# The first load in two halves: x tile 0 from two queues, and the loads behind it moved on ScalarE's queue

## The chip, the cores and the metric

The kernel runs on one core of one Trainium2 chip, in one launch. The metric is the device time in microseconds. The trace comes from one profiled execution; times without a profile come from repeated runs. The engines are TensorE (PE; its weight loads are shown as PEld), VectorE (DVE), ScalarE (ACT), GpSimd (POOL) and SyncE (SP). SyncE, ScalarE and GpSimd also issue DMAs; in the packet lists SyncE's queue is q1 and ScalarE's is q10.

## The reference

```python
def _A_ref(x, wqkv, w_phi, wo):              # S=2048 tokens, D=448, 16 heads of 28
    q, k, v = split_heads(x @ wqkv)
    pq, pk = q @ w_phi, k @ w_phi            # per head
    phi_q = concat(softmax(pq), softmax(-pq))
    phi_k = concat(softmax(pk), softmax(-pk))
    kv  = einsum("bhsf,bhsd->bhfd", phi_k, v)
    z   = einsum("bhsf->bhf", phi_k)
    num = einsum("bhqf,bhfd->bhqd", phi_q, kv)
    den = einsum("bhqf,bhf->bhq", phi_q, z) + 1e-6
    return merge_heads(num / den) @ wo

def _B_ref(x, w1, w2):                       # w1 448x1792, w2 1792x448
    return silu(x @ w1) @ w2

xn = layernorm(x)                            # over D, eps 1e-5
return x + _A_ref(xn, ...) + _B_ref(xn, ...)
```

Everything is bf16; the input x is (1, 2048, 448).

## The kernel before

The 2048 tokens are 16 tiles of 128 rows (x tile t, 112 KB each). Tiles 0 to 3 are loaded one by one, the rest in blocks of four. Each tile is normalised on VectorE (`ln_tile`, L717): statistics (`bnst`, L720), mean and variance (`bnag`, L721), the reciprocal of the root (`rstd`, L726; the root itself, `ve`, L724, runs on ScalarE for tiles 0 to 3), and the normalised tile (`xn`, L735). Tiles 0 to 3 are then transposed on TensorE (`tr`, L539) into PSUM and copied out to `xnT` by ScalarE (`ev`, L545), tile 3 by VectorE; later tiles are transposed by DMA. On `xnT` the first feed-forward product starts at once, for tokens 0 to 511, in pieces per tile (L522): `00a` is block 0 on tile 0, first two steps.

The program is written as a list of operations with the ranges they read and write. A planner (`schedule`, L228) books each on its engine with a duration from small formulas and a landing time for loads, and so fixes each engine's order; semaphore waits follow from the ranges. `chain` (L1036) adds order edges by name, within one engine. The order of TensorE is wholly written out: the word list at L1062 for the head, a plan string (L361) for the rest. For VectorE's head it is L1047, for ScalarE's L1048.

Before any data arrive, 36 matmuls on a constant run on TensorE (L588, traced as L589), and an `act` on `ones_bf` (L568, named `warm_act`) brings ScalarE's square-root table in; the planner books it with n = 2050, where `d_act(n)` (L509) is n/1.2 + 60 ns. `ones_bf` is set by a GpSimd memset named `ones`.

The first loads (L605 to L608): x tile 0 from SyncE, then tiles 1, 2 and 3 from ScalarE. Behind tile 0 SyncE issues the blocks of `w1` (traced as `phT`, in whose space they lie), then the other weights and x blocks, which wait for nothing. On ScalarE the order is x1, x2, the table warm-up, x3; and x1 waits for `ones` (L1050):

```python
chain("bnst0 bnag0 bnst1 rstd0 bnag1 xn0 rstd1 xn1 bnst2 bnag2 bnst3 bnag3 rstd2 xn2 ...".split())
chain("x1 x2 warm_act x3 ve0 ve1 ev0a ev0 ev1a ev1 ve2 ve3 ev2a ev2 silu_table".split())
byname["x1"].deps.add(byname["ones"].id)
for name, lat in (("x1", 2000.0), ("x2", 2800.0), ("x3", 2200.0)):
    byname[name].xfer, byname[name].lat = 0.0, lat
```

So tile 1's statistics stand ahead of xn0 on VectorE, and tile 2's behind xn1. The last two of these lines are the planner's landing times for x1, x2 and x3.

Of the kernel before, what the change touches and what calls it, by code (L numbers as in the profile page):

```python
# [370 lines left out]
def bass_parallel_sum__linear_kernel_hedgehog__dense_activation_silu__prompt_kernel(  # L371
# [29 lines left out]
    def rows_of(a, t0, t1):  # L401
        for u0, u1 in TILES:
            if u0 <= t0 < u1:
                v = a[0][128 * u0:128 * u1, :].rearrange("(p t) d -> p t d", p=128)
                return v[:, t0 - u0:t1 - u0, :]
# [3 lines left out]
    with es:  # L409
        def sb(name, shape, dt):  # L410
            return es.enter_context(nc.sbuf_tensor(name, shape, dt))

        x_sb = sb("x_sb", [128, NT, D], BF16)
# [64 lines left out]
        warm_act = sb("warm_act", [128, 4], F32)  # L478
# [76 lines left out]
        def load(dst, src, name, eng="sp", lat=1700.0):  # L555
            n = 2
            for _, cnt in list(dst.ap):
                n *= cnt
            P.dma(lambda e: e.dma_start(out=dst, in_=src), n / 280.0, writes=[dst], name=name, eng=eng, lat=lat)
# [35 lines left out]
        def load_x(t0, t1, eng="sp"):  # L595
            load(x_sb[:, t0:t1, :], rows_of(A_x, t0, t1), f"x{t0}", eng, lat=1400.0)
# [5 lines left out]
        def load_w1(c0, c1, eng="sp"):  # L602
            load_rows4(w1_sb[:, :, c0:c1], B_w1, c0, c1, f"w1_{c0}", eng)

        load_x(0, 1)  # L605
        load_x(1, 2, "act")
        load_x(2, 3, "act")
        load_x(3, 4, "act")  # L608
# [427 lines left out]
        def chain(names):  # L1036
            byname = {o.name: o for o in P.ops}
            for a, b in zip(names, names[1:]):
                byname[b].odeps.add(byname[a].id)
                byname[b].odeps -= byname[b].deps  # L1040
# [4 lines left out]
        fold()  # L1045
        act(warm_act[:], ones_bf[:, 0:4], ACTF.Silu, 4, "silu_table", table="silu", okeys_w=["sq"])
        chain("bnst0 bnag0 bnst1 rstd0 bnag1 xn0 rstd1 xn1 bnst2 bnag2 bnst3 bnag3 rstd2 xn2 rstd3 xn3 ev3".split())  # L1047
        chain("x1 x2 warm_act x3 ve0 ve1 ev0a ev0 ev1a ev1 ve2 ve3 ev2a ev2 silu_table".split())  # L1048
        byname = {o.name: o for o in P.ops}
        byname["x1"].deps.add(byname["ones"].id)  # L1050
        for name, lat in (("x1", 2000.0), ("x2", 2800.0), ("x3", 2200.0)):
            byname[name].xfer, byname[name].lat = 0.0, lat
        fold_loads()
# [239 lines left out]
```

## Time and profile before

| | us |
|---|---|
| median of 3 runs | 144.71 (144.23, 144.71, 145.35) |
| the profiled execution | 144.79, of which the span is 143.5 |
| TensorE busy | 140.7 (98% of the span) |
| VectorE, ScalarE, GpSimd busy | 90.3, 79.6, 78.8 |
| x tile 0: issued, landing after | 0.80, 2.1 |
| x tile 1: issued, landing after | 1.04, 2.1 |
| first w1 block (256 KB): issued, landing after | 1.27, 3.9 |
| x tile 2 and x tile 3: landing after | 3.7 and 3.7 |

Times of instructions count from the span's start. A timeline row gives the start, the length from first to last of a merged group, engine, line, operation, output and inputs, the number of instructions, and in brackets the idle time ahead of it and what ended it. A merged row of two loads covers both. A matmul's row ends when its result is out; matmuls overlap, so their number in a stretch tells more than the busy share.

### The profile page before, as it was taken

Reading aid. Unit: us, or ns where it says so; the run is one execution under the profiler, and the core shown is the slowest. Engines: PE = TensorE matmul, PEld = TensorE weight load, DVE = VectorE, ACT = ScalarE, POOL = GpSimd, SP = SyncE. Lnnn points to the kernel's source line nnn. Section 1 sums busy time; section 2 is a strip of 40 time slices with the busy share of each in tenths; the row PEclk is TensorE's granted clock in tenths of the full one; section 3 lists DMA queues with packets and bytes.
Section 4 is the critical chain, followed back from the end, with each engine's and each line's share of the span. In section 5 each row is a group of like instructions: output and inputs, shape, how many; then the busy total and the mean of one; then the engine's idle time right before and its main releaser. Section 6 shows DMA issues by size and latency. Waiting matters only on the chain.

```text
span 143.5 us, 4565 instructions
## 1 busy us (share of the span) xinstructions
PE 140.7 (98%) x1966; PEld 82.8 (58%) x1966; DVE 90.3 (63%) x194; ACT 79.6 (55%) x98; POOL 78.8 (55%) x98
## 2 busy tenths in 40 slices
PE   7999999999999999999999999999999999999994
PEld 7894444445444544476687655555555555555673
DVE  1978998700860069939049998957977564265533
ACT  4668776479996999889888948237440000000000
POOL 8948667570296009799935999991595700000000
DMA  4999998675990000000000058959589999824922
GB/s 126 328 308 262 275 165 116 117 100 95 350 286 5 0 2 5 0 0 5 0 5 5 5 106 163 138 109 159 106 164 144 215 214 162 144 49 97 181 83 64
DMA packets 45252, 17.43 MB, mean 121 GB/s; under 512 B 37024, under 2 KB 44848, under 8 KB 45232
## 3 DMA queue, kind: packets, MB, share of 16 engines
q1 hardware_dynamic: 42160, 14.35, 53.9%
q10 hardware_dynamic: 2736, 2.14, 5.8%
q0 software_dynamic: 336, 0.65, 1.3%
q8 instruction: 15, 0.25, 0.7%
q14 instruction: 5, 0.04, 0.1%
HBM read 6.40 MB, written 1.84 MB: 57 GB/s over the span
## 4 chain that ended last, share of the span: by engine, by line
PE 98%; DVE 0%; issue 0%
PE psum L522 94%; PE psum L589 3%; PE psum L539 1%; DVE x_sb L1023 0%
## 5 line engine op out<-in xcount | busy, mean ns | idle before, releaser
L522 PE MATMUL psum<-xnT,phT 64*128 64x512 bf16 (+1 forms) x428 | 47.0, 351 | 0.0
L522 PE MATMUL psum<-w_sb,hT 64*128 64x448 bf16 (+4 forms) x455 | 46.0, 340 | 0.0
L856 DVE TENSOR_REDUCE Rec<-Ek_sb 128x32 f32<-128x896 bf16 (+1 forms) x20 | 24.6, 1258 | 18.6 <-ACT Ek_sb L545 18.6
L522 PEld LDWEIGHTS psum<-w_sb,hT 64*128 64x128 bf16 (+1 forms) x455 | 23.6, 94 | 17.5 <-ACT Ek_sb L545 0.2
L545 ACT ACTIVATE hT<-psum 128x1024 bf16<-128x1024 f32 x28 | 27.6, 1024 | 10.6 <-PE psum L522 10.5
L522 PEld LDWEIGHTS psum<-xnT,phT 64*128 64x128 bf16 (+1 forms) x428 | 22.8, 95 | 17.6 <-ACT vaug L545 0.7
L893 POOL TENSOR_TENSOR RA<-Ek_sb,Rec 128x896 bf16<-128x896 bf16 x16 | 26.6, 1698 | 6.3 <-DVE Rec L857 4.7
L522 PE MATMUL psum<-Wqk,xnT 64*128 64x432 bf16 x224 | 24.6, 343 | 0.0
L545 ACT ACTIVATE Ek_sb<-psum 128x864 bf16<-128x864 f32 x24 | 20.4, 913 | 6.3 <-PE psum L522 5.4
L866 POOL TENSOR_TENSOR Ek_sb<-Ek_sb,Rec 128x896 bf16<-128x896 bf16 x8 | 13.4, 1698 | 15.9 <-DVE Rec L857 8.8
L545 ACT ACT_TABLE_LOAD x11 | 14.1, 1283 | 2.8 <-POOL Wp L552 1.9
L522 PEld LDWEIGHTS psum<-Wqk,xnT 64*128 64x128 bf16 x224 | 10.9, 94 | 8.1 <-ACT hT L545 0.4
L866 POOL TENSOR_TENSOR phT<-phT,Rec 128x896 bf16<-128x896 bf16 x8 | 13.4, 1698 | 1.2 <-issue 0.9
L522 PE MATMUL psum<-wv,xnT 64*128 64x448 bf16 x112 | 12.4, 349 | 0.0
L720 DVE BATCH_NORM_STATS2 st<-x_sb 128x6 f32<-128x448 bf16 x16 | 9.6, 602 | 2.9 <-DMA x_sb<-in_A_x_dram 2.9
L522 PE MATMUL psum<-wo_sb,vaug 64*128 64x448 bf16 (+2 forms) x102 | 11.3, 339 | 0.0
L1023 DVE TENSOR_TENSOR x_sb<-psum,x_sb 128x448 bf16<-128x448 f32 (+2 forms) x13 | 7.2, 584 | 5.6 <-PE psum L522 5.5
L735 DVE TENSOR_SCALAR RA<-x_sb,mv,rstd 128x384 bf16<-128x384 bf16 (+2 forms) x28 | 9.5, 376 | 0.7 <-POOL rstd L731 0.5
L1002 DVE TENSOR_TENSOR vaug<-psum,rden 128x448 bf16<-128x448 f32 x16 | 9.3, 620 | 0.0
L856 DVE TENSOR_REDUCE Rec<-phT 128x64 f32<-128x1792 bf16 x4 | 8.0, 1991 | 1.9 <-ACT phT L545 1.8
L857 DVE RECIPROCAL Rec<-Rec 128x32 f32<-128x32 f32 (+1 forms) x24 | 8.9, 397 | 0.2
L545 ACT ACTIVATE vaug<-psum 128x896 bf16<-128x896 f32 x8 | 7.5, 949 | 2.4 <-PE psum L522 2.4
(61 smaller groups left out, 109.3 us busy)
## 6 DMA issues: line engine op xcount, KB each, us to landing
out_dram<-x_sb ACTq DMA_DIRECT2D x15, 112.0 KB, 2.6
w_sb<-in_B_w_dram SPq DMA_DIRECT2D x1, 1568.0 KB, 7.4
x_sb<-in_A_x_dram SPq DMA_DIRECT2D x2, 448.0 KB, 6.7
wo_sb<-in_A_wo_dram SPq DMA_DIRECT2D x2, 336.0 KB, 7.2
phT<-in_B_w_dram SPq DMA_DIRECT2D x3, 192.0 KB, 5.4
x_sb<-in_A_x_dram POOLq DMA_DIRECT2D x1, 448.0 KB, 4.6
phT<-in_B_w_dram SPq DMA_DIRECT2D x1, 384.0 KB, 6.3
x_sb<-in_A_x_dram ACTq DMA_DIRECT2D x3, 112.0 KB, 3.7
```

Source lines behind the costliest of these rows:

```text
L522: r = e.matmul(dst, lhsT, rhs, start=st, stop=sp, skip_group_check=True)
L539: r = e.transpose(dst, src, ident[:])
L545: P.op("act", d_act(n), lambda e: e.activation(dst, src, func, scale=scale), reads=[src], writes=[dst], table=table, name=name, **keys)
L589: o = P.op("pe", 107.0, lambda e: e.matmul(banks[3][:, 0:128], unit, unit, start=True, stop=True), reads=[], writes=[banks[3][:, 0:128]], ...
L720: P.op("dve", 590, lambda e: e.bn_stats(st6[:, t, :], xs), reads=[xs], writes=[st6[:, t, :]], name=f"bnst{t}", okeys_w=["ln"])
L735: P.op("dve", dur, lambda e: e.tensor_scalar(dst, x_sb[:, t, c0:c1], mv[:, t, 0:1], rstd[:, t:t + 1], ALU.subtract, ALU.mult), reads=[xs, ...
L856: P.op("dve", 50 + 967 * n, lambda e: e.tensor_reduce(R2, E4, AXL.X, ALU.add), reads=[E4], writes=[R2], name=f"Ssum_{tag}")
L857: P.op("dve", 135 + 210 * n, lambda e: e.reciprocal(R2, R2), reads=[R2], writes=[R2], name="Rrec")
L866: P.op("pool", 1700, lambda e: e.tensor_tensor(E3, E3, Rk.rearrange("p (h s) -> p h s", s=2)[:, :, :, None].broadcast_to([128, H, 2, DH]), ...
L893: P.op("pool", 1700, lambda e: e.tensor_tensor(dst, Eq, Rq.rearrange("p (h s) -> p h s", s=2)[:, :, :, None].broadcast_to([128, H, 2, DH]) ...
L1002: P.op("dve", 620, lambda e: e.tensor_tensor(o3, U3[:, :, 0:DH], rden[:, uq, :, None].broadcast_to([128, H, DH]), ALU.mult), reads=[U3[:, ...
L1023: P.op("dve", d_dve(cs.stop - cs.start), lambda e: e.tensor_tensor(res[:, cs], ob, addend[:, cs], ALU.add), reads=[ob, addend[:, cs]], wri ...
```

## The change

x tile 0 is loaded by two DMAs of 64 rows, rows 0 to 63 from SyncE as before and rows 64 to 127 from ScalarE (`x0b`). On ScalarE `x0b` is the first issue, x1 follows it without the wait for `ones`, the table warm-up comes next, then x2 and x3. The planner's landing times for x1, x2 and x3 stay.

```diff
-        load_x(0, 1)
+        for i, (name, eng) in enumerate((("x0", "sp"), ("x0b", "act"))):
+            rows = slice(64 * i, 64 * i + 64)
+            load(x_sb[rows, 0:1, :], rows_of(A_x, 0, 1)[rows], name, eng, lat=1400.0)
         load_x(1, 2, "act")
         load_x(2, 3, "act")
         load_x(3, 4, "act")
...
-        chain("x1 x2 warm_act x3 ve0 ve1 ev0a ev0 ev1a ev1 ve2 ve3 ev2a ev2 silu_table".split())
+        chain("x0b x1 warm_act x2 x3 ve0 ve1 ev0a ev0 ev1a ev1 ve2 ve3 ev2a ev2 silu_table".split())
         byname = {o.name: o for o in P.ops}
-        byname["x1"].deps.add(byname["ones"].id)
         for name, lat in (("x1", 2000.0), ("x2", 2800.0), ("x3", 2200.0)):
             byname[name].xfer, byname[name].lat = 0.0, lat
```

## The prediction

> **What bounds the kernel now.** I read the page first: busy shares, then the chain that ended last.
>
> ```profile
> span 143.5 us, 4565 instructions
> ...
> PE 140.7 (98%) x1966; PEld 82.8 (58%) x1966; DVE 90.3 (63%) x194; ACT 79.6 (55%) x98; POOL 78.8 (55%) x98
> ...
> PE 98%; DVE 0%; issue 0%
> ```
>
> TensorE is on the chain for 98% of the span, so a change in the first loads counts only as far as it moves TensorE. The chain in order of time shows where that can be:
>
> ```profile
> 0.84 4.00 PE psum L589 x36
> 4.84 0.09 issue
> ...
> 8.81 132.81 PE psum L522 x1852
> ```
>
> The 36 warm-up matmuls (L589, no input) fill 0.84 to 4.84 us; from 8.81 one unbroken piece runs to the last output. What can move is the head between. The timeline of the first 9 us shows its links (start, duration, engine):
>
> ```profile
> 0.80 0.41 SPq L559 DMA_DIRECT2D x_sb<-in_A_x_dram  x1
> ...
> 1.04 0.86 ACTq L559 DMA_DIRECT2D x_sb<-in_A_x_dram  x2
> ...
> 1.27 1.98 SPq L559 DMA_DIRECT2D phT<-in_B_w_dram  x4
> ...
> 2.93 0.63 DVE L720 BATCH_NORM_STATS2 st<-x_sb 128x6 f32<-128x448 bf16 x1 [2.93 <-DMA x_sb<-in_A_x_dram]
> ...
> 3.69 0.59 DVE L720 BATCH_NORM_STATS2 st<-x_sb 128x6 f32<-128x448 bf16 x1
> ...
> 4.90 0.35 PEld L539 LDWEIGHTS psum<-ident,RA 128*128 128x128 bf16 x4 [0.33 <-issue]
> ...
> 5.37 0.62 DVE L720 BATCH_NORM_STATS2 st<-x_sb 128x6 f32<-128x448 bf16 x1
> ...
> 5.51 0.34 PEld L539 LDWEIGHTS psum<-ident,RA 128*128 128x128 bf16 x4 [0.26 <-DVE RA L735]
> ...
> 7.23 0.40 DVE L735 TENSOR_SCALAR RA<-x_sb,mv,rstd 128x448 bf16<-128x448 bf16 x1
> ...
> 7.81 0.27 PEld L539 LDWEIGHTS psum<-ident,RA 128*128 128x128 bf16 x4
> ```
>
> Tile 0 starts the statistics at 2.93, and VectorE then works in a fixed order: statistics of tile 1 (3.69), xn0 (4.42 to 4.78), xn1 (ends 5.46), statistics of tile 2 (5.37), xn2 (7.23 to 7.63). Each xn frees a transposition: weight loads at 4.90, 5.51 and 7.81. The two idle notes, 0.33 and 0.26, are nearly all that TensorE loses.
>
> Two windows of TensorE (start:end, length, busy with matmul count, clock, DMA) show something else:
>
> ```profile
> 5.90:6.40 0.50, 0.50 (x8) 1.00 1.07 389
> 6.60:7.10 0.50, 0.50 (x13) 1.00 0.90 316
> ```
>
> The same 128x128 matmul comes at half pace before about 6.5 us (the warm-ups: 36 in 4.00, 111 ns each) and at nearly twice that pace after it (8 against 13 touch a half microsecond, those that reach in from outside counted), although the granted clock reads 1.00 in both. Time won before 6.5 us is thus worth about half.
>
> **x0 in two halves.** 112 KB from SyncE become 56 KB each from SyncE and ScalarE. Issue to landing of x0 was 2.1 us (0.80 to 2.9). Do halves move side by side? Packets per queue (q1 SyncE, q10 ScalarE) in 1.8 to 2.2, 2.4 to 2.6 and 2.8 to 3.2 us:
>
> ```profile
> q1 hardware_dynamic: 85, 0.08, 71.8%
> ...
> q10 hardware_dynamic: 72, 0.06, 90.6%
> ...
> q1 hardware_dynamic: 69, 0.07, 69.2%
> ```
>
> x0 has the engines alone (no q10 packet before 2.2, though x1 was issued at 1.04), then x1, then the first w1 block, in order of issue. Whole transfers follow one another here; two halves would too, and the second would end where x0 ended. Bounds: x0's packets spread over 1.8 to 2.55, so perfectly parallel halves land up to 0.37 sooner; if ScalarE can issue no earlier than its 1.04 of now, 0.24 later. That wait was for `ones` (a GpSimd memset, 0.80 to 1.00), which the half doesn't read, so 0.80 is likely. I take 0. The statistics wait for two landings instead of one: 0 to 0.09 (the step on ScalarE's queue between x2's issue end, 1.90, and x3's, 1.99, across the warm-up); I take 0.
>
> The Trainium skill ("DMA: Bandwidth & Descriptors", Rules for kernel authors) speaks against the change: two transfers to disjoint partition halves serialize, use one of 128 partitions. By it x0 gains nothing, as in the packet rows; by perfect halves the sum would be the parallel rival's.
>
> **x1 behind the half.** x1's issue loses the wait for `ones` and gains an issue in front. ScalarE's issues take 0.43 (0.86 for two), so x1 goes out near 0.80 + 0.43 = 1.23 instead of 1.04, only 0.04 ahead of the w1 block at 1.27. If it stays ahead, it lands at 1.23 + 2.1 = 3.3, before the 3.69 at which VectorE takes it: cost 0. If it falls behind, that is the first rival.
>
> **Warm-up before x2.** The table load (1.28 us) moves from 1.93 to about 1.7; x3 was issued at 1.99 while it ran, so it doesn't hold the queue. ScalarE's first root starts at 3.81, after the warm-up either way: worth 0. The cover is that wait for tile 0's statistics; were they done before 3.2, the table load would show. x2 goes out at 1.23 + 0.43 + 0.09 = 1.75 instead of 1.47, and x3 at 2.2 instead of 1.99. Both took 3.7 us to land, so x2 moves from 5.1 to 5.4; ends: 5.1 (no change) and 5.7 (x3's landing now, should x2 fall behind the second w1 block, issued near 1.74). VectorE wants x2 at 5.37 and xn2 follows it rigidly. xn1's end and its weight load lie 0.05 apart, so tile 2 was ready at 7.68 against 7.81: slack 0.13. x2 at 5.4 costs bnst2 0.07, inside the slack; at 5.7, 0.36 - 0.13 = 0.23. Being nearer the early end, but with every transfer around it shifted, I take 0.1. x3 at 5.9 is still ahead of its 6.12: 0. Queued behind x1, x2 and x3 on ScalarE are its roots and evacuations, none before 3.8, so later issues (done by 2.6) hold up nothing. SyncE's queue keeps its order: a half need not be issued faster than x0's 0.41. GpSimd's queue is passed by nothing.
>
> **Sum.** 0 + 0 + 0 + 0.1 = +0.1 us on the profiled execution's 144.79 (span 143.5 and 1.29 around it; 0.08 above the median of 144.71): 144.9. Cases with the same words but other ends give 144.7 to 145.1.
>
> **Rivals.**
> *Slower: x1 falls behind the first w1 block.* It decides if x1's packets start after w1's; the margin is 0.04 us. For it: issue order ruled. x1 would land as x2 did, 3.7 after issue: 4.9. VectorE's order puts tile 1's statistics before xn0, so xn0, xn1 and xn2 all slip by 4.9 - 3.69 = 1.2 at most; at tile 2, less 0.13, TensorE loses 1.1: up to 145.9, mostly 145.2 to 145.9. But TensorE would then stand idle from 4.84 to about 6.1, just while its pace is still half. *The pace is earned late* is the worse branch: the step at 6.5 came 1.6 us after the first transposition and 5.6 after the first warm-up. Counted anew from 6.1 it falls between 7.7 and 11.7, and half pace from 6.5 on costs half of 1.2 to 5.2: 0.6 to 2.6, middle 1.6, of which the waiting for tile 2 hides some. Together +1.7 to +2.6: 146.5 to 147.4.
> The Trainium skill ("TensorE: Matmul & The Clock Gate", Part 1) has a free-running window of 3.4 us that must be busy before the clock doubles; a failed window would by it cost 1.7 us, and its phase alone would spread runs of one kernel. The one trace can't show the phase; the three times before do spread by 1.12 us.
>
> *Faster: the halves move side by side.* Then x0 lands 0.37 sooner. The warm-ups hold TensorE until 4.8 anyway, x1's 3.3 limits xn1 to about 0.33 sooner, and at half pace this is worth 0.15. Tile 2 caps it: with x2 at 5.1 at best, xn2 is ready 0.2 sooner. 144.4 to 144.7, say 144.6. Against it stand the packet rows.
>
> *Another order of work.* The planner books the warm-up as 2050/1.2 + 60 = 1768 ns on ScalarE, so it believes that x2 now goes out at 3.5 instead of 1.3 and lands at 6.8 instead of 4.5, and plans xn2 and what follows about 1 us later, while loads stay put. The order of TensorE is written out, those of ScalarE, VectorE and GpSimd only in part; another choice there can put waits into the unbroken 132.81 us, or take out what small gaps are in it. Nothing in the trace prices this: from -1.6 (the head's 0.6 idle and about 1 us of half pace and gaps) to +3, i.e. 143.1 to 147.8.
>
> **How the numbers follow.** Forecast 0.34 (144.7 to 145.1); side by side 0.16; x1 behind with the pace kept 0.13; x1 behind and the pace late 0.17; another order 0.20, of which 0.11 slower by over 1%, 0.03 within and 0.06 faster. 1% is 1.45 us, about what the three runs' spread lets one tell from no change. Faster by over 1%: 0.06. Slower: 0.17 + 0.11 = 0.28. Within: 0.66. The range runs from 144.0 (the parallel case at its best, with the spread of runs below it) to 147.0, leaving out the tails of the reordering and the late pace.
>
> **What would show it.** Right: tile 0's statistics again near 2.9, x1's packets ahead of the w1 block's, weight loads of the first transposition near 4.9 and of tile 2 near 7.9, half pace ending near 6.5. x1 behind: tile 1's statistics after 4. Side by side: statistics before 2.7 and both queues' packets mixed at 1.8 to 2.2. Another order: pieces of waiting in the chain after 9 us. Wrong altogether: if ScalarE's half is issued late, or if the pace changes at another time in a way that nothing on TensorE before it explains.

## The result, and the profile after

The changed kernel took 147.22 us in the median of six runs (145.72 to 147.52); the kernel before, run beside it, 144.75 (144.23 to 145.35). The ratio is 1.015 with a 95% interval from 1.011 to 1.019: slower by about 1.5%. The profiled execution took 145.72, of which the span is 144.5. Of all runs below, one, 148.36 with the old order on ScalarE, lies over 1.5% above the fastest of its kernel and counts in no ratio.

Two things show in the six times: the lowest is 1.5 us below the median, and nothing lies between 146.16 and 147.21. The kernel has two groups of times, and the profiled execution belongs to the lower one. So there are two questions: what costs 0.9 us in the profiled execution (145.72 against 144.79), and what costs 1.5 us more in the others.

The head of the chain of waits of the kernel after, in order of time (start, length, what):

```profile
0.82 0.57 ACTq L559
1.39 0.04 issue
1.42 3.65 DMA x_sb<-in_A_x_dram
5.07 0.02 issue
5.10 0.63 DVE st L722
...
6.50 0.41 DVE RA L737
...
9.87 132.67 PE psum L522 x1853
```

Before, the 36 warm-ups opened this chain. Now it begins with the issue of tile 0's second half on ScalarE, and goes on with x1's load, which lands only at 5.07; VectorE takes tile 1's statistics (L722, which was L720) at 5.10. The unbroken piece at the end is as long as before (132.67 against 132.81 us): the loss is in the head, all of it. The timeline of the same execution:

```profile
0.81 0.58 SPq L559 DMA_DIRECT2D x_sb<-in_A_x_dram  x1
0.82 1.46 ACTq L559 DMA_DIRECT2D x_sb<-in_A_x_dram  x2
...
1.45 2.12 SPq L559 DMA_DIRECT2D phT<-in_B_w_dram  x4
...
3.33 0.63 DVE L722 BATCH_NORM_STATS2 st<-x_sb 128x6 f32<-128x448 bf16 x1 [3.33 <-DMA x_sb<-in_A_x_dram]
...
5.10 0.63 DVE L722 BATCH_NORM_STATS2 st<-x_sb 128x6 f32<-128x448 bf16 x1 [0.93 <-DMA x_sb<-in_A_x_dram]
...
6.37 0.38 PE L539 MATMUL psum<-ident,RA 128*128 128x128 bf16 x4 [1.53 <-DVE RA L737]
```

Tile 0's statistics start at 3.33 instead of 2.93, tile 1's at 5.10 instead of 3.69, and the first transposition at 6.37 instead of 4.93: 1.44 us later. TensorE stands idle for 1.53 us after its warm-ups. Then the pace, from a window of 0.5 us (start:end, length, busy with matmul count, clock, DMA):

```profile
7.50:8.00 0.50, 0.50 (x13) 1.00 1.10 339
```

13 matmuls are the full pace. In this execution it is there from the first transposition on, while before it came only at about 6.5. The profiled time less the start of the first transposition is 139.35 here and was 139.9 before: the half pace had cost some 0.5 us, and this is why a start 1.44 us later costs 0.93 in the end.

Where x1 was, the packets per queue tell (count, MB, share of the 16 DMA engines' time; q1 is SyncE, q10 ScalarE), in 2.0 to 2.4, 2.6 to 2.9, 2.9 to 3.5 and 3.5 to 3.9 us:

```profile
q1 hardware_dynamic: 46, 0.04, 37.5%
...
q10 hardware_dynamic: 50, 0.03, 36.6%
...
q1 hardware_dynamic: 95, 0.10, 68.4%
...
q1 hardware_dynamic: 113, 0.11, 77.7%
q10 hardware_dynamic: 26, 0.02, 17.2%
```

The half of SyncE comes first, then mostly that of ScalarE, then from 2.9 to 3.5 the w1 block alone, and x1 only from about 3.5. Yet x1's issue began at 1.42 and the w1 block's at 1.45: it began first and was served second. It also took longer and so ended later, at 2.28 against 2.01 (the tiles' views of the two issues, in ns):

```profile
L559 ACTq DMA_DIRECT2D x_sb<-in_A_x_dram x1: 857/857/857, 1.4 to 1.4; - x1
```

```profile
L559 SPq DMA_DIRECT2D phT<-in_B_w_dram x1: 567/567/567, 1.4 to 1.4; - x1
```

### The profile page after: what moved, and what is told of

It is laid out like the page before. It is cut to its first block, busy times and chain, and to the rows that moved or that the text cites. A ratio compares the mean times of both kernels' runs of the same rounds, so it can differ in the third digit from the quotient of the medians.

```text
span 144.5 us, 4567 instructions
## 1 busy us (share of the span) xinstructions
PE 140.0 (97%) x1966; PEld 81.6 (56%) x1966; DVE 90.1 (62%) x194; ACT 79.6 (55%) x98; POOL 78.7 (54%) x98
## 3 DMA queue, kind: packets, MB, share of 16 engines
HBM read 6.40 MB, written 1.84 MB: 57 GB/s over the span
## 4 chain that ended last, share of the span: by engine, by line
PE 94%; DMA 3%; DVE 1%; ACTq 0%; ACT 0%; issue 0%
PE psum L522 93%; DMA x_sb<-in_A_x_dram 3%; PE psum L539 1%; DVE st L722 0%; ACTq L559 0%; DVE RA L737 0%; DVE x_sb L1025 0%; ACT ve L726 0%; DVE rstd L728 0%; DVE mv L723 0%
## 5 line engine op out<-in xcount | busy, mean ns | idle before, releaser
L545 ACT ACTIVATE hT<-psum 128x1024 bf16<-128x1024 f32 x28 | 27.6, 1024 | 10.6 <-PE psum L522 10.6
L522 PEld LDWEIGHTS psum<-Wqk,xnT 64*128 64x128 bf16 x224 | 10.6, 94 | 8.4 <-ACT hT L545 0.4
L722 DVE BATCH_NORM_STATS2 st<-x_sb 128x6 f32<-128x448 bf16 x16 | 9.7, 605 | 4.6 <-DMA x_sb<-in_A_x_dram 4.6
```

The costliest lines, as they stand in the source:

```text
L522: r = e.matmul(dst, lhsT, rhs, start=st, stop=sp, skip_group_check=True)
L545: P.op("act", d_act(n), lambda e: e.activation(dst, src, func, scale=scale), reads=[src], writes=[dst], table=table, name=name, **keys)
L722: P.op("dve", 590, lambda e: e.bn_stats(st6[:, t, :], xs), reads=[xs], writes=[st6[:, t, :]], name=f"bnst{t}", okeys_w=["ln"])
```

## The experiments

The theory formed from this: with loads waiting on both queues, the SDMA engines start one load of SyncE, then one of ScalarE, and so on in turn. The order of starts before was x0 (SyncE), x1 (ScalarE), w1, x2; now it is x0, its second half, w1, x1. The half takes ScalarE's first turn, and x1 gets the place that x2 had: it landed at 5.07, x2 before at 5.13. The rivals: the order in which the issues begin, lost by a hair; a late or long issue of x1 itself; another cause than the loads. There is one rival more, which no run below was built to tell from the turns: the order in which the issues end. It too has x1 behind the w1 block now (2.28 against 2.01) and ahead of it before (1.42 against 1.69). For the two groups of times the theory is that TensorE's pace changes late where it stands idle for 1.5 us ahead of its work.

### The changed kernel again

> The changed kernel once more, with another profile. If the loss has two parts (x1 late: always about +1.0 us; half pace lasting on because TensorE stood idle: 0 to +1.7 us, by chance of each run), times fall between 145.6 and 147.6 and the profile's time goes with the moment at which 128x128 matmuls go from 107 to 56 ns apart: about +0.5 us of time for each us that the moment lies later than 6.4. If the times above 146 come from another place, the head of this profile looks like the first one (change of pace before 6.4) whatever its time is.

145.82 us (145.64 to 147.22, six runs), ratio 1.009 with an interval from 1.004 to 1.015. With the first six runs that makes six at 145.64 to 146.16 and six at 147.00 to 147.52. The two medians of one kernel, 147.22 and 145.82, differ by how many runs fell into each group.

### Is it the moment of issue?

Three kernels move it. The first makes SyncE's first w1 block wait for a memset (the edit is on the kernel after):

```diff
+        byname["w1_0"].deps.add(byname["wp_zero"].id)
+        byname["w1_0r"].odeps.add(byname["w1_0"].id)
```

> Halves and the order on ScalarE as in the change, but SyncE's first w1 block waits for a GpSimd memset that ends near 1.8, so x1's issue has no rival. If x1 falling behind the w1 block is the cause: x1 lands near 3.4, tile 1's statistics start by 4.0, the first transposition by 5.2, and the time is 144.7 to 145.3. If the late x2 (behind the warm-up) is the cause, x2 still lands near 5.8 or later and the time stays at 145.7 or above. If a new order of work is the cause, the time also stays at 147.

146.56 us (146.01 to 147.13, four runs), 1.013 (1.008 to 1.018). The w1 issue moved only to 1.82, inside x1's own issue (1.42 to 2.28), and x1 landed at 5.35. So x1's issue began 0.40 ahead and w1's packets still came first (2.89): the order in which issues begin is not the rule. Between turns and the order of the ends (2.26 for w1, 2.28 for x1) this hold decides nothing. The second puts the wait for `ones` back, on the half:

```diff
+        byname["x0b"].deps.add(byname["ones"].id)
```

> The changed kernel, but ScalarE's half of x tile 0 waits for `ones` and so is issued near 1.04 instead of 0.82, after SyncE's half has got away. In the change x1's issue took 0.86 us (1.42 to 2.28) with or without a w1 block beside it. If it is the two first issues at one moment that block ScalarE's queue: the half's issue and x1's take about 0.4 each, x1 lands by 3.8, the first transposition comes near 5.2 and the time is 144.7 to 145.5. If it is the extra half in front of x1 on ScalarE as such: x1's issue is again 0.8 or longer, x1 lands near 5 and the time is 145.6 to 147.5.

146.44 us (145.71 to 147.19, four runs), 1.014 (1.008 to 1.019). The half was now issued 0.24 behind SyncE's, at 1.04, and x1 at 1.61; still x1 landed at 5.07 and the first transposition came at 6.36, as in the kernel after. That both loads start in one moment is not the cause. The third holds the w1 block longer and keeps SyncE's loads behind it in order:

```diff
+        byname["w1_0"].deps.add(byname["mask_half"].id)
+        loads = [o for o in P.ops if o.is_dma and o.eng == "sp"]
+        for p, o in zip(loads, loads[1:]):
+            o.odeps.add(p.id)
+            o.odeps -= o.deps
```

> The change, but SyncE's first w1 block waits for the GpSimd memset and mask work that ends near 3.14, so that its issue certainly comes after x1's (which ended at 2.28); the order of SyncE's loads is kept. If x1's packets stand behind the w1 block's in the change: now they start near 2.9 on ScalarE's queue, x1 lands at 3.6 to 4.2, xn0 ends by 5.3 and the first transposition starts by 5.4. If x1's own issue of 0.86 us, and not the w1 block, is what delays it: its packets start near 3.5 again and it lands at 4.2 or later. The time tells less, since the w1 block now lands near 5.5 to 6.5 and the first feed-forward matmuls may wait for it: 144.9 to 146.5.

146.59 us (146.19 to 147.43, four runs), 1.016 (1.013 to 1.020). First its timeline, then its packets from 2.9 to 3.5:

```profile
0.82 1.46 ACTq L559 DMA_DIRECT2D x_sb<-in_A_x_dram  x2
...
3.19 1.98 SPq L559 DMA_DIRECT2D phT<-in_B_w_dram  x4
...
5.36 0.38 PE L539 MATMUL psum<-ident,RA 128*128 128x128 bf16 x4 [0.52 <-DVE RA L737]
...
9.06 0.51 PE L522 MATMUL psum<-xnT,phT 128*128 128x128 bf16 x6 [1.32 <-DMA phT<-in_B_w_dram]
```

```profile
q10 hardware_dynamic: 141, 0.12, 73.6%
```

ScalarE issues exactly as in the kernel after (0.82, 1.46 long for both loads), but with nothing of SyncE waiting x1's packets fill the stretch that was w1's. x1 landed at 3.90 and the first transposition moved from 6.37 to 5.36. So 1.01 of the 1.44 us is the w1 load in x1's way, ahead of it and then beside it, and x1's long issue (0.86 us for one load) alone doesn't keep its packets back. Whether the long issue is why x1 came second to w1 is not shown: here w1's issue began only at 3.19, so x1 comes first under either rule. The time doesn't fall, since w1 is now missing at 9.06: the hold is a probe, not a cure.

### Which queue has x1, which tile goes first

In the next kernel x1 rides behind the half on SyncE, ahead of the w1 blocks:

```diff
-        load_x(1, 2, "act")
+        load_x(1, 2, "sp")
...
-        chain("x0b x1 warm_act x2 x3 ve0 ...".split())
+        chain("x0 x1 w1_0 w1_0r".split())
+        chain("x0b warm_act x2 x3 ve0 ...".split())
```

> The halves as in the change, but x1 is issued by SyncE behind its half and ahead of the first w1 block; ScalarE issues its half, then the warm-up, x2 and x3. (Holding the w1 block to 1.82 was no test: its issue still ended at 2.26, 0.02 ahead of x1's, and its packets still went first.) If x1's packets standing behind the w1 block's are what delays it: x1's packets now start near 2.9, x1 lands by 4.0, xn0 ends by 5.2, the first transposition starts by 5.4 and the time is 144.7 to 145.6. If the halves delay x1 in another way (whatever queue it goes by): x1 lands at 4.7 or later and the time is 145.6 or more.

145.18 us (144.93 to 146.66, seven runs), 1.008 (1.004 to 1.011). x1 landed at 4.63, between the two forecasts of 4.0 and 4.7: first came x2 (4.26), in ScalarE's turn, and also with the earlier end of issue (1.99 against 2.27). A better place on its own queue did not bring x1 ahead of the other queue's next load. The next one takes the kernel before and drops only the line that makes x1 wait for `ones`:

```diff
-        byname["x1"].deps.add(byname["ones"].id)
```

> The kernel before with one line gone: x1 doesn't wait for `ones`, so whole x0 (SyncE) and whole x1 (ScalarE) are issued at one moment; no halves, order x1, x2, warm-up, x3. If two first issues at one moment are the cause: both issues take about 0.57 as in the change, and the next one on ScalarE, x2's, takes about 0.86, so x2 lands near 5.4 or later; x0 or x1 lands up to 0.3 later than 2.9 and 3.2; the time is 144.8 to 146.0. If the halves are the cause: all issues take about 0.4, x1 lands near 3.0 and the time is as before, 144.2 to 145.4.

144.91 us (144.75 to 146.76, ten runs), 1.005 (1.002 to 1.008). Here x1's packets went first (1.84) and x0's followed (2.01); they landed at 3.40 and 3.58, and tile 0's statistics slid from 2.93 to 3.60:

```profile
3.60 0.63 DVE L720 BATCH_NORM_STATS2 st<-x_sb 128x6 f32<-128x448 bf16 x1 [3.60 <-DMA x_sb<-in_A_x_dram]
...
5.60 0.38 PE L539 MATMUL psum<-ident,RA 128*128 128x128 bf16 x4 [0.77 <-DVE RA L735]
```

This was not foreseen, and it is useful: the wait for `ones`, which the change also removes, had kept x1 from going ahead of x0, as it did in this profile. Two of the ten runs, 146.39 and 146.76, lie in an upper group here too.

### What the half itself costs

Both row halves from SyncE, on the kernel before:

```diff
-        load_x(0, 1)
+        for i, name in enumerate(("x0", "x0b")):
+            rows = slice(64 * i, 64 * i + 64)
+            load(x_sb[rows, 0:1, :], rows_of(A_x, 0, 1)[rows], name, "sp", lat=1400.0)
```

> The kernel before with x tile 0 in two halves, both issued by SyncE one behind the other; ScalarE's order and x1's wait for `ones` as before. If halves cost only their extra issue: the second half lands 0.3 to 0.5 later than whole x0 did, tile 0's statistics start near 3.3, x1 lands near 3.2 to 3.6, the first transposition comes near 5.2 to 5.4 and the time is 144.8 to 145.4 with the pace as before. If halves as such put x1 behind: x1 near 5 and 145.6 to 147.5.

146.34 us (145.67 to 146.85, four runs), 1.013 (1.009 to 1.017). x1 landed at 3.64, between the halves, and now the second half was late, at 3.97. The first transposition came at 6.07, not at the forecast's 5.2 to 5.4, and the time is above the 144.8 to 145.4 that went with it. Each half takes 0.57 to 0.58 us to issue. The issue of x0 on SyncE in the tile's view (ns, start), before and after:

```profile
L559 SPq DMA_DIRECT2D x_sb<-in_A_x_dram x1: 412/412/412, 0.8 to 0.8; - x1
```

```profile
L559 SPq DMA_DIRECT2D x_sb<-in_A_x_dram x1: 580/580/580, 0.8 to 0.8; - x1
```

Half the bytes take 0.17 us longer to issue. To see whether it is the size or the form, the next kernel halves tile 0 by columns, all 128 rows each:

```diff
-            rows = slice(64 * i, 64 * i + 64)
-            load(x_sb[rows, 0:1, :], rows_of(A_x, 0, 1)[rows], name, eng, lat=1400.0)
+            cols = slice(224 * i, 224 * i + 224)
+            load(x_sb[:, 0:1, cols], rows_of(A_x, 0, 1)[:, :, cols], name, eng, lat=1400.0)
```

> The change with x tile 0 cut by columns instead of rows: two loads of 128 rows x 224 columns, the same bytes each, from the same queues at the same moment; all else as in the change. If the 64-row form is slow to issue (0.57 against 0.41, and its packets 1.36 after the issue against 1.04): issues take about 0.4 again, x1 is issued near 1.24 to 1.7, its packets go ahead of the w1 block's or mix with them, x1 lands by 4.2 and the time is 144.8 to 145.7. If any three loads in quick succession do it: x1's issue takes 0.8 or more, x1 lands near 5 and the time is 145.6 to 147.5. Against both: packets of 448 bytes are twice as many, which can make both halves land 0.1 to 0.4 later.

146.81 us (145.31 to 147.09, four runs), 1.013 (1.010 to 1.017). The start of its timeline, and its packets from 2.0 to 2.4:

```profile
0.80 0.41 ACTq L559 DMA_DIRECT2D x_sb<-in_A_x_dram  x1
...
1.24 0.48 ACTq L559 DMA_DIRECT2D x_sb<-in_A_x_dram  x1
...
1.28 1.97 SPq L559 DMA_DIRECT2D phT<-in_B_w_dram  x4
```

```profile
q1 hardware_dynamic: 101, 0.04, 44.6%
q10 hardware_dynamic: 97, 0.04, 39.7%
```

The long issue is gone (0.41 and 0.42), so it belongs to the form of 64 rows and not to the bytes. The two halves truly run side by side, and land at 2.92 and 3.11: no sooner than the whole x0 at 2.90. And x1, whose issue began at 1.24, the prediction's margin of 0.04 ahead of w1's 1.28, still started behind w1 (first packets at 2.58 and 2.37); then the two loads mixed, and x1 landed at 4.65, later than the 4.2 forecast for short issues. This refutes, a second time, the order in which issues begin. The order in which they end is not refuted: w1's ended at 1.71 and x1's at 1.72, a difference too small to build on.

### The warm-up's place on ScalarE

On the kernel after, x2 ahead of the table warm-up as it was before:

```diff
-        chain("x0b x1 warm_act x2 x3 ve0 ...".split())
+        chain("x0b x1 x2 warm_act x3 ve0 ...".split())
```

> The halves as in the change, but x2 ahead of the table warm-up as before (x0b, x1, x2, warm-up, x3). If the warm-up's move is harmless (x2 leaves only 0.1 us later for it): the same time as the change, 146.5 to 147.5, x1 landing near 5.1. If x2's place is the cause: 145 or less.

147.21 us (145.71 to 147.31, three runs), 1.014 (1.007 to 1.020); x1 at 5.45. In these runs the warm-up's move neither caused the loss nor eases it.

### The two groups: TensorE's pace

More warm-ups on the kernel after, with the same loads, so that TensorE is busy for longer before tile 0 arrives:

```diff
-        for i in range(36):
+        for i in range(50):
...
+        byname["tr0a"].odeps.update(o.id for o in P.ops if o.name == "warm")
```

> The changed kernel with 50 warm-up matmuls instead of 36, so that TensorE is busy until about 6.4 (or until the pace has changed); the loads are as in the change. If the half pace lasting on behind the idle stretch is the second part of the loss: the runs near 147.2 go, the median is 145.4 to 146.0. If x1's lateness alone is the loss: the median stays at 147.2. Should the extra warm-ups themselves hold up the first transposition, it starts after 6.5 in the profile and the time rises by as much.

And fewer of them on the kernel before, whose loads stay untouched:

```diff
-        for i in range(36):
+        for i in range(24):
```

> The kernel before with 24 warm-up matmuls instead of 36: loads and order untouched, but TensorE stands idle for 1.5 us ahead of the first transposition, as in the change. If the idle stretch alone makes the pace change late in some runs: times from 144.2 to 146.6, median 145.0 to 146.0, and a profiled run of 146 or more shows half pace beyond 8. If idle time ahead of the data is harmless: 144.2 to 145.4 as before.

With 50: 145.88 us (145.83 to 146.24, four runs), 1.008 (1.005 to 1.011), and no run near 147. With 24: 146.00 (144.37 to 146.46, five runs), 1.011 (1.008 to 1.014), four of the five 1.5 to 2.1 us above the lowest. The profiled run with 24 is that lowest one. Its timeline shows the idle stretch, 1.28 us, that the kernel before doesn't have:

```profile
0.85 2.72 PE L589 MATMUL psum<-const-bfloat16-1.0 128*128 128x128 bf16 x24 [0.85 <-PEq L1278]
...
4.85 0.38 PE L539 MATMUL psum<-ident,RA 128*128 128x128 bf16 x4 [1.28 <-DVE RA L735]
```

So idle time ahead of the first transposition brings the second group with no load moved, and filling it made the second group vanish in four runs (if half the runs fell there by chance, four of four would be spared once in 16). With 24, TensorE is also busy for less time in all (2.7 us instead of 4.0), which this run doesn't tell apart from the idle stretch. And the kernel before isn't quite free of such times: of its 55 runs on record one took 146.12. What the second group looks like inside shows in the profile of the kernel with the old order on ScalarE, 147.31 us, in two windows:

```profile
9.00:9.50 0.50, 0.50 (x7) 1.00 1.03 266
10.60:11.00 0.40, 0.40 (x11) 1.00 1.14 310
```

At 9.0 TensorE still works at half pace (7 matmuls in 0.5 us); the full pace comes at 10.0, where the kernel after had it before 6.4. Its trace and that of the first hold (full pace from 9.75, 147.13 us) are the two that caught this. There is a second way into the upper group, seen in the column halves' profile: the pace is there and is lost again for 3.4 us (the last section). That run's mean granted clock is 0.988; of the changed kernel's six upper runs two have the same 0.988, and four have 1.00, as the old order's profile has.

Last, 40 warm-ups on the kernel before, to see whether it leaves anything to win there:

```diff
-        for i in range(36):
+        for i in range(40):
```

> The kernel before with 40 warm-up matmuls instead of 36, which closes the idle stretch of about 0.3 us ahead of the first transposition. If only an idle stretch of about 1.5 us makes the pace late, and 0.3 us is too short for it: the time stays within 0.3 us of before, 144.3 to 144.9 at the median. If 0.3 us already does it in part of the runs: the median falls by 0.2 to 0.5 and runs above 145 go. The four extra matmuls can hold up the first transposition by 0.1 to 0.2 us at half pace.

144.52 us (144.44 to 144.98, twelve runs), 1.0005 (0.9995 to 1.0014): no difference. No kernel beat the one before.

## Why the prediction was right and wrong

The forecast of 144.9 fell. What came was its first rival, x1 behind the first w1 block, in both branches: the lower group, 145.64 to 146.16, is nearly the branch with the pace kept (145.2 to 145.9), the upper, 147.00 to 147.52, nearly the one with the pace late (146.5 to 147.4). The first six runs' median of 147.22 lies 0.2 above the range; the middle of all twelve, between 146.16 and 147.00, lies in it. The two branches had 0.13 and 0.17 where the forecast had 0.34. So it is the rivals that brought the range up to the measured time, not the path that was forecast, and on which side of 147.0 a median falls is the luck of how many runs land in each group.

One table holds the steps together. Where the full pace is there before the first transposition and nothing later waits, the profiled time less that start is 139.35 to 139.6:

| kernel | x1 landed | first transposition | full pace from | time | time less start |
|---|---|---|---|---|---|
| before | 3.19 | 4.93 | 6.5 | 144.79 | 139.9 |
| after | 5.07 | 6.37 | before it | 145.72 | 139.35 |
| 50 warm-ups | 4.96 | 6.25 | 4.7 | 145.83 | 139.6 |
| x1 at once | 3.40 | 5.60 | before it | 145.11 | 139.5 |
| 24 warm-ups | 3.08 | 4.85 | before it | 144.37 | 139.5 |
| old order | 5.45 | 6.96 | 10.0 | 147.31 | 140.35 |
| column halves | 4.65 | 5.95 | 3.8, but half from 7.2 to 10.6 | 147.09 | 141.1 |

- *"If it stays ahead, it lands at 1.23 + 2.1 = 3.3 ... cost 0."* This step failed. The packet rows of before were read as order of issue, and they fit that; they fit turns between the queues just as well, and turns would have put x1 behind w1 whatever the margin. They also fit the order in which issues end, and by that x1 fell behind because its issue took 0.86 where the sum had 0.43. Nor was x1 issued at 1.23: behind a half whose issue took 0.57, its own began at 1.42, still just ahead of w1's 1.45. The column halves had short issues and the margin of 0.04, and x1 was behind. The w1 load in x1's way costs 1.01 of the start's 1.44 us (from the long hold). The Trainium skill ("DMA: Bandwidth & Descriptors", Queues, rings and completion order) has each SDMA engine go round its queues packet by packet; here no ScalarE packet came from 2.9 to 3.5, with x1's issue ended at 2.28, and later packets did mix (113 beside 26). Either whole loads took turns at their start, or x1's packets were not yet there to be served; no run tells which.
- *"I take 0"* for the halves: that they gain nothing was right, that they cost nothing was not. Statistics start 0.40 later (3.33 against 2.93), outside the bound of 0.24. The term missed was the issue: 0.57 to 0.58 for a half against 0.41 for the whole, and packets from 2.17 instead of 1.84. "A half need not be issued faster" was said; slower wasn't thought of.
- *Side by side* fell as a gain: the column halves do mix, and land with the whole x0 at best. The Trainium skill ("DMA: Bandwidth & Descriptors", Rules for kernel authors), cited in the prediction, has two partition halves serialize. The packets of the row halves agree, SyncE's ahead of ScalarE's; the price of the halves here was 0.40 us.
- *Warm-up before x2, 0.1 us:* harmless, as predicted, but for another reason than given: x2 landed at 5.80 and was not the latest any more, since tile 1 was.
- *Another order of work* fell: one unbroken piece of TensorE, 132.67 us against 132.81.
- *The pace:* that time won before 6.5 is worth about half was roughly right, since a start 1.44 later cost 0.93. That the pace would be late if TensorE stood idle was right in about half the runs; the upper group then lies 1.5 us above the lower (medians of the six runs in each: 147.22 and 145.75).

What stays open: why a load of 64 rows takes longer to issue, and why x1's issue behind it takes 0.86 us. Whether that long issue lost x1 its place or whether the queues take turns is open too: both are inferred from the order of starts, both fit these traces, and no run separates them. A run in which x1's issue ends clearly ahead of w1's, while both then wait to start, would. Nor was the changed kernel itself profiled in its upper group: in the two profiles that stand in for it, about 1.0 us is pace (140.35 and 140.5 against 139.4 in the last column), and 0.3 to 0.6 is a first transposition at 6.65 and 6.96, since x1 landed later there (5.35 and 5.45), for a reason that no run singles out.

## What to carry to other kernels

A new small load is not free for the loads behind it on its queue: here it put the load that mattered behind a 256 KB block of the other queue, although that block's issue began later. Whether to count loads per queue or the ends of their issues isn't settled here, so look at both. Before splitting a load, look at what its issue costs in the new form, and at which row of the timeline the second piece displaces. If a change delays the first matmul, let the warm-ups reach up to it, or count the pace lost as part of the price.

## What the runs showed of the hardware

The pace can be lost again after it has been earned. In the column halves' profile the windows read (start:end, length, busy with count, clock, DMA):

```profile
3.80:4.20 0.40, 0.40 (x10) 1.00 1.01 333
6.70:7.20 0.50, 0.50 (x12) 0.98 1.00 356
8.00:8.50 0.50, 0.50 (x7) 0.50 1.13 341
10.60:11.10 0.50, 0.50 (x12) 1.00 1.14 263
```

Full pace from 3.78, no matmul started between 4.19 and 5.95, half pace from 7.23, full again from 10.62: the turns are 3.45 and 3.39 us apart. The Trainium skill ("TensorE: Matmul & The Clock Gate", Part 1) has a free-running window of about 3.4 us, and the trace agrees. The trace's own clock records agree more closely, with turns at 3.77, 7.18 and 10.59, 3.41 us apart. In the ten other traces that have such records the full clock lasts 139.95 or 136.53 us, which is 41 or 40 times 3.413. So a turn falls on a grid of its own in each execution: in the changed kernel's profile at 5.47 and in its repeat at 4.96, both while TensorE was idle, and in the two profiles with the late pace at 9.71 and 9.97. That the two groups of times come from where this grid lies against the idle stretch fits all of these; no run could set it.

The Trainium skill's table on the same page ("TensorE: Matmul & The Clock Gate", Why this matters for your kernels) allows gaps of up to about 3 us. Here one of 1.76 us from start to start was enough, while in the changed kernel's profile one of 1.84 us cost no pace behind it. The granted clock shows only one of the two kinds of half pace: 0.50 at 8.0, when it had been lost, but 1.00 in the old order's 9.0 to 9.5, where it had not yet been earned. The old order's clock records begin at 9.97, and the kernel before has none, so the 1.00 ahead of the first record is no reading. Counting matmuls in a window shows both.
